# Rounding the second MLP's weights during attention, by way of DRAM, in an attention-and-two-MLPs kernel

## The chip, the cores and the metric

One core of one Trainium2 chip runs the whole kernel. The metric is device time in microseconds (us), the median of the runs shown. TensorE is called PE, VectorE DVE, ScalarE ACT, GpSimd POOL; SP is the queue of SyncE, which issues every DMA of this kernel.

## The reference

```python
# q, k, v: (4, 8, 768, 64) float32; chunks of 32 queries, 16 keys left, 8 keys right, 8 memory keys
scores = scale * np.matmul(q_c, k_full.transpose(0, 1, 3, 2))
a = softmax(scores)
out[:, :, c_start:c_end] = np.matmul(a, v_full)
x = out.transpose(0, 2, 1, 3).reshape(3072, 512)
h = np.maximum(np.maximum(x @ w1, x @ w2), x @ w3)     # d_ff 768
x = h @ w_out
h = x @ w_in                                           # d_ff 2048
g = np.where(h >= 1, h, np.where(h <= -1, 0, (h + 1) ** 2 / 4))
out = g @ w_out2
```

All six weight matrices are float64.

## The kernel before

**Work.** The 3072 tokens form 24 units of 128 for attention and 6 blocks of 512 (`TB`) for the products. Every product is made of float32r parts, hi and lo, as three matmuls (`mm3`, L467). One *slot* (l1, l2, l3 or l4) is 12 matmuls of 512 columns. The first MLP takes 24 slots a block: for each of six f, l1 with m = 0, l1 with m = 1, l2 of the f before, l1 with m = 2. An l1 result in one of two PSUM buffers is read by ACT for m = 0 (L492) and by DVE for m = 1, 2 (L494, `l1_max`); after m = 2, ACT makes hi (L477) and POOL lo (L478). The second MLP follows for all six blocks: 96 slots l3 (`slot_l3`) and 96 slots l4.

**Weights.** A float64 weight tile of 512 KB is fetched into one of three `st` buffers (`fetch_w`, L106) and converted: `convert_w` (L120) makes a float32 bit pattern from the upper word on DVE (L129 absolute value, L130 clamp, L131 shift and mask, L133 sign), `hi_w` rounds it to float32r on ACT (L140), `rest_w` (L143) takes the lower word's share on DVE (L146, L152), `lo_w` subtracts and adds on POOL (L159, L160). The 24 tiles of the first MLP ("a", "b") are converted in block 0, the 32 of the second ("c", "d") from the start of the last block on: `w_step` (L584) does one whole tile, in the loop over the last block's slots (L692) and before l3 slots (L706 to L710). The 48 weight buffers hold 24 tiles in hi and lo; 16 more are made where attention's buffers lay, once attention is done (L685).

**Order.** Units 0 to 7 and block 0 follow a list written out by hand. After that every engine's queue holds the program's order: for each slot of blocks 1 to 4 (96 slots) the slot itself, then one step of attention (`att_step`, L461). `steps` (L432 on) gives each unit u six steps: 0 scores and softmax start, 1 and 2 normalising and preparing keys and queries of later units, 3 transposing probabilities, 4 their product with v (`st_o`), 5 transposing the result into `xh`, `xl` (L410, L414). From unit 12 on keys and queries are transposed by DVE (`flip_k` L296, `flip_q` L302) from buffers that `load_ks` (L271) and `load_qs` (L286) fill three units at a time, with 20 and 16 DMAs; `load_v` fills the one buffer `vw` with 8 DMAs, in step 4. In units 12 and later a unit's step 2 is: `flip_k` of the next unit, `flip_q` of the one after that, then the loads.

```python
if last_block:
    t = s - last_block
    if t % 3 != 2 and converted[0] - 32 < t:
        w_step()
...
else:
    att_step()
```

Of the kernel before, what the change touches and what calls it, by code (L numbers as in the profile page):

```python
# [1 line left out]

# [16 lines left out]
P = 128  # L19
CH = 32          # queries per chunk  # L20
LEFT = 16        # context keys left of a chunk
RIGHT = 8        # context keys right of a chunk
NM = 8           # memory keys
WIN = LEFT + CH + RIGHT
NK = NM + WIN    # keys a chunk attends to
NC = P // CH     # chunks per unit of 128 tokens
TB = 512         # tokens per block
UB = TB // P     # units per block
FLOOR = -3.0e38
TRIO0 = 12       # first unit whose queries and keys the vector engine transposes  # L30
# float32 patterns of a float64's upper word at float32's smallest and largest exponents
LEAST, MOST = 2.0 ** -15, float.fromhex("0x1.dffffep+16")

# Order of the parts of units 0 to 7 and of block 0's products, by name and number: loads (lk lq lv
# lm lmem, f: weights), units (tk ck ek kw tq c0q c1q mem mv s mx ex n a ca o co x cx dx), weights (wa
# wh wg wp), products (l lt lh m), d: matrix products that only keep the tensor engine's clock up.
# The tensor engine follows it as it stands; it sets the priorities on the other engines.
# [18 lines left out]
# what the vector engine copies instead of ScalarE, and which steps go from it to another engine  # L56
# [11 lines left out]
def attention_then_two_mlps(ctx, tc, q, k, v, mem_k, mem_v, w1, w2, w3, w_mid, w_in, w_out, out):  # L68
# [4 lines left out]
    KD = DM // P          # 4  # L73
    K1 = F1 // P          # 6
    K2 = F2 // P          # 16
    HP = H // 2           # head pairs
    UPB = S // P          # units per batch
# [17 lines left out]
    yd = dram.tile([DM, NT], F32, name="yd")  # L95

    # ---------------------------------------------------------------- weights
    # A float64 weight comes as two 32-bit words.  It is kept as two float32r parts: `hi`
    # rounds the float32 that the upper word gives, `lo` holds the rest, the lower word's
    # share included.  # L100
# [19 lines left out]
    def convert_w(kind, j):  # L120
        st = staged.pop((kind, j))
        low, up = st[:, :, 0], st[:, :, 1]
        c = stage.tile([P, TB], U32, tag="c", name=f"c_{kind}_{j}")
        cf = c.bitcast(F32)
        V = nc.vector
        if f"{kind}.{j}" in ABS_ON_ACT:
            nc.scalar.activation(out=cf, in_=up.bitcast(F32), func=AF.Abs)
        else:
            V.tensor_scalar(out=c, in0=up, scalar1=0x7FFFFFFF, scalar2=None, op0=ALU.bitwise_and)  # L129
        V.tensor_scalar(out=cf, in0=cf, scalar1=LEAST, scalar2=MOST, op0=ALU.max, op1=ALU.min)  # L130
        V.tensor_scalar(out=c, in0=c, scalar1=3, scalar2=0x3FFFFFFF,  # L131
                        op0=ALU.logical_shift_left, op1=ALU.bitwise_and)
        V.scalar_tensor_tensor(out=c, in0=up, scalar=0xC0000000, in1=c,  # L133
                               op0=ALU.bitwise_and, op1=ALU.bitwise_or)
        half[kind, j] = low, up, c
# [26 lines left out]
    # ---------------------------------------------------------------- attention  # L162
    kTb = [at.tile([P, HP, LEFT + P + RIGHT], F32, name=f"kTb{i}") for i in range(2)]
# [93 lines left out]

    # From unit TRIO0 on, three units at a time, the loads put a head's parity and half of its
    # dims in a partition's quadrant, so that transposes of 32 x 32 blocks are all that is left.
    # Blocks of keys start LEFT tokens before a chunk.  # L260
    NB3 = 3 * NC
    ks = kq[:, 0:HP * (NB3 + 1) * CH].rearrange("p (h c d) -> p h c d", h=HP, d=CH)
    qs = {}

# [6 lines left out]
    def load_ks(g):  # L271
        b, s0 = divmod(3 * g, UPB)
        t0 = s0 * P - LEFT
        c0 = 1 if t0 < 0 else 0
        for h in range(HP):
            for r, a in quadrants(k[b], h, t0 + c0 * CH, CH, NB3):
                nc.sync.dma_start(out=ks[r:r + CH, h, c0:c0 + NB3, :], in_=a)
        r0, c, t = (LEFT, 0, 0) if c0 else (0, NB3, S - LEFT)
        for e in range(2):
            for x in range(2):  # L280
                r = (2 * e + x) * 32 + r0
                nc.sync.dma_start(
                    out=ks[r:r + LEFT, :, c, :],
                    in_=k[b].rearrange("(h e) t d -> e t h d", e=2)[e, t:t + LEFT, :, 32 * x:32 * x + 32])

    def load_qs(g):  # L286
        b, s0 = divmod(3 * g, UPB)
        for i in range(2):
            t = stage.tile([P, TB, 2], U32, tag="st", name=f"qs{g}_{i}", bufs=3)
            qs[g, i] = t.rearrange("p f t -> p (f t)").bitcast(F32)[:, 0:2 * NB3 * CH].rearrange(  # L290
                "p (h c d) -> p h c d", h=2, d=CH)
            for h in range(2):
                for r, a in quadrants(q[b], 2 * i + h, s0 * P, CH, NB3):
                    nc.sync.dma_start(out=qs[g, i][r:r + CH, h], in_=a)

    def flip_k(u):  # L296
        c = u % 3 * NC
        fill_mk(u)
        nc.vector.transpose(out=kw[:, :, :, NM:NM + CH], in_=ks[:, :, c:c + NC, :])
        nc.vector.transpose(out=kw[:, :, :, NM + CH:], in_=ks[:, :, c + 1:c + 1 + NC, :])  # L300

    def flip_q(u):  # L302
        c = u % 3 * NC
        for i in range(2):
            for e in range(2):
                r = slice(e * 64, e * 64 + 64)
                nc.vector.transpose(
                    out=qTb[u % 2][r, 2 * i:2 * i + 2, :, e, :], in_=qs[u // 3, i][r, :, c:c + NC, :])

    # the two heads of a pair lie on the diagonal of a block of queries  # L310
# [6 lines left out]
    # rows of a score tile: (chunk parity, head parity, query); columns: (chunk pair, head pair, key),  # L317
    # with the head pairs in the order 0, 2, 1, 3
# [51 lines left out]
    # heads g and g + 4 share the partitions of a transposed tile, g = 2 * (pair % 2) + parity  # L370
# [54 lines left out]
    def steps(u):  # L425
# [13 lines left out]
        if u >= TRIO0 - 3 and u % 3 == 0:  # L439
            v += [("gq", u // 3 + 1)]  # L440
# [7 lines left out]
        yield v + [("lv", u + 1)]  # L448
        yield [("x", u), ("cx", u), ("dx", u)]

    def run(kind, i):
        if kind in ("gk", "gq"):
            if i < NU // 3:
                parts[kind](i)
        elif kind in ("lm", "f", "d", "wa", "wh", "wg", "wp") or i < NU:
            parts[kind](i)
# [4 lines left out]
    def att_step():  # L461
        if todo:
            for s in todo.pop():
                run(*s)

    # ---------------------------------------------------------------- products
# [38 lines left out]
    def slot_l2(j, f):  # L505
        hi, lo = hs.pop(("A", j, f))
        whi, wlo = weights["b", f]
        for d in range(KD):
            if f == 0:
                acc[d] = ps_acc.tile([P, TB], F32, tag=f"acc{d}", name=f"y{j}_{d}")  # L510
            c = slice(d * P, (d + 1) * P)
            mm3(acc[d], whi[:, c], wlo[:, c], hi, lo, f == 0, f == K1 - 1)
            if f == K1 - 1:
                pool, tag = (mx, "y") if d < 2 else (bp["p"], "y") if bp else (stage, "c")
                y = pool.tile([P, TB], F32, tag=tag, name=f"y_{j}_{d}", bufs=2)
                nc.scalar.copy(out=y, in_=acc[d])
                nc.sync.dma_start(out=yd[d * P:(d + 1) * P, j * TB:(j + 1) * TB], in_=y)
# [16 lines left out]
    def slot_l3(i, f):  # L534
# [5 lines left out]
        # with u = max(h/2 + 1/2, 0) the gate is max(min(u, 1) * u, h)  # L540
# [26 lines left out]
    # ---------------------------------------------------------------- schedule  # L567
# [11 lines left out]
    def w_fetch():  # L579
        while fetched[0] < min(converted[0] + 3, len(conv)):  # L580
            fetch_w(*conv[fetched[0]][0])
            fetched[0] += 1

    def w_step():  # L584
        if converted[0] == len(conv):
            return
        w_fetch()
        n, pool = conv[converted[0]]
        pool = pool or bp["w"]
        convert_w(*n)  # L590
        hi_w(*n, pool)
        rest_w(*n)
        lo_w(*n)
        converted[0] += 1
        w_fetch()

    later = ExitStack()
    with tc.manual_schedule(engines={ENG.PE}), later:
# [8 lines left out]
        # what no load or copy writes of the buffers that stay  # L607
# [5 lines left out]
        # until the first products two buffers of later blocks serve, too  # L613
# [23 lines left out]
        # keeps the tensor engine's clock up while it waits for the first units  # L637
# [41 lines left out]
        for s, (f, *a) in enumerate(order):  # L679
# [9 lines left out]
            if last_block:  # L689
                t = s - last_block  # L690
                # a slot of the last block frees its weights' tiles
                if t % 3 != 2 and converted[0] - 32 < t:  # L692
# [8 lines left out]
            else:  # L701
                att_step()
        for f, *a in orderB:
            if f is slot_l3:
# [3 lines left out]
                if i == 0:  # L708
                    for _ in range({0: 0, 1: 0, 5: 2, 7: 2}.get(ff, 1)):
                        w_step()  # L710
# [39 lines left out]
```

## Time and profile before

| what | value |
|---|---|
| median of 3 runs | 1139.43 us (1139.12 to 1139.65) |
| span of the profiled execution, first to last instruction | 1136.8 us |
| its own time | it is not listed apart from the three runs; the median is 2.6 us over the span |
| PE busy | 1051.1 us, 92% of the span |
| DVE / ACT / POOL busy | 599.0 / 326.2 / 392.3 us |
| mean granted TensorE clock | 0.973 |

A busy share is a mean over stages: attention's head and block 0 (to about 170 us), blocks 1 to 4 with the rest of attention (to 479 us), the last block with the weight conversion (to about 700 us), and the second MLP. Matmuls overlap in the records, so the time of one slot is read from their starts and not from the sum of their durations.

### The profile page before, as it was taken

What the parts mean: (1) busy time and instruction counts of PE and PEld (TensorE: products, weight loads), DVE (VectorE), ACT (ScalarE), POOL (GpSimd) and SP (SyncE); (2) the same over time, 40 slices, a digit from 0 to 9 for tenths busy, and PEclk for the clock granted to TensorE, in tenths of its full rate; (3) what the DMA queues carried; (4) which work ended last, traced back from release to release, by engine and by line L of the source; (5) the groups of instructions that cost most, each with busy time, mean ns of one, the idle gap of its engine ahead of it and who ended that gap; (6) DMA issues with size and microseconds to landing.
All of it is one profiled execution on the core that took longest, in us unless ns stands there. A gap on an engine that the chain in (4) does not pass through costs nothing.

```text
span 1136.8 us, 15111 instructions
## 1 busy us (share of the span) xinstructions
PE 1051.1 (92%) x5890; PEld 848.2 (75%) x5890; DVE 599.0 (53%) x875; ACT 326.2 (29%) x608; POOL 392.3 (35%) x297
## 2 busy tenths in 40 slices
PE   5887789999999999987888779999999999999998
PEld 4765577888878888866666567888888888888886
DVE  8899963444435343399989996222222222222222
ACT  5734342232222222222132223222222222222222
POOL 5465650001000001166666664332332232232221
PEclk8998999999999999998988899999999999999999
DMA  8655423224233320243233221001001000000101
GB/s 203 171 135 139 111 67 87 52 42 91 44 60 80 57 73 18 71 138 104 93 109 104 84 65 47 19 10 47 10 19 47 10 19 29 28 10 1 37 1 37
DMA packets 154774, 72.94 MB, mean 64 GB/s; under 512 B 125264, under 2 KB 142672, under 8 KB 154704
## 3 DMA queue, kind: packets, MB, share of 16 engines
q1 hardware_dynamic: 154704, 71.99, 23.9%
q8 instruction: 46, 0.75, 0.3%
q14 instruction: 24, 0.20, 0.1%
HBM read 59.38 MB, written 12.58 MB: 63 GB/s over the span
## 4 chain that ended last, share of the span: by engine, by line
PE 69%; DVE 25%; issue 3%; DMA 1%; ACT 1%; POOL 0%; SPq 0%; DVEq 0%; POOLq 0%; ACTq 0%
PE l L468 13%; PE l L469 13%; PE l L470 13%; PE o L557 7%; PE o L556 7%; PE o L555 6%; PE y L468 2%; DVE u L543 2%; PE y L469 2%; PE y L470 2%; DVE c_d L130 2%; PE s L326 2%; DVE c_c L130 2%; PE o L389 2%; DVE c_d L129 1%
## 5 line engine op out<-in xcount | busy, mean ns | idle before, releaser
L543 DVE SCALAR_TENSOR_TENSOR u<-u 128x512 f32<-128x512 f32 x96 | 82.5, 859 | 316.0 <-ACT u L542 316.0
L478 POOL TENSOR_TENSOR hl_b<-u,hh_b 128x512 fp32r<-128x512 f32 x96 | 124.1, 1293 | 317.7 <-ACT hh_b L477 183.9
L468 PE MATMUL l<-xh,hi_a 128*128 128x512 f32 x432 | 178.0, 412 | 20.7 <-DVE t L494 20.7
L468 PE MATMUL l<-yh,hi_c 128*128 128x512 f32 x384 | 155.2, 404 | 26.3 <-DVE u L544 21.3
L470 PE MATMUL l<-xh,lo_a 128*128 128x512 f32 x432 | 171.3, 397 | 0.3 <-POOL lo_a L160 0.3
L469 PE MATMUL l<-xl,hi_a 128*128 128x512 f32 x432 | 171.0, 396 | 0.0
L469 PE MATMUL l<-yl,hi_c 128*128 128x512 f32 x384 | 153.8, 400 | 0.0
L470 PE MATMUL l<-yh,lo_c 128*128 128x512 f32 x384 | 153.7, 400 | 0.0
L555 PE MATMUL o<-hi_d,hh_b 128*128 128x512 f32 x384 | 150.0, 391 | 0.0
L557 PE MATMUL o<-hi_d,hl_b 128*128 128x512 f32 x384 | 150.0, 391 | 0.0
L556 PE MATMUL o<-lo_d,hh_b 128*128 128x512 f32 x384 | 149.9, 390 | 0.0
L478 POOL TENSOR_TENSOR hl_a<-t,hh_a 128x512 fp32r<-128x512 f32 x36 | 48.6, 1351 | 286.2 <-ACT hh_a L477 286.2
L542 ACT ACTIVATE u<-l 128x512 f32<-128x512 f32 x96 | 57.3, 596 | 204.3 <-PE l L470 168.8
L468 PEld LDWEIGHTS l<-xh,hi_a 128*128 128x128 f32 x432 | 83.1, 192 | 41.1 <-DVE t L494 24.5
L468 PEld LDWEIGHTS l<-yh,hi_c 128*128 128x128 f32 x384 | 73.9, 192 | 46.7 <-DVE u L544 25.4
L477 ACT CAST hh_b<-u 128x512 fp32r<-128x512 f32 x96 | 59.6, 621 | 158.5 <-DVE u L544 158.5
L494 DVE TENSOR_TENSOR t<-l,t 128x512 f32<-128x512 f32 x72 | 49.6, 689 | 104.1 <-PE l L470 99.8
L470 PEld LDWEIGHTS l<-xh,lo_a 128*128 128x128 f32 x432 | 82.6, 191 | 18.9 <-POOL lo_a L160 0.7
L469 PEld LDWEIGHTS l<-xl,hi_a 128*128 128x128 f32 x432 | 83.2, 193 | 15.7
L470 PEld LDWEIGHTS l<-yh,lo_c 128*128 128x128 f32 x384 | 74.3, 193 | 16.8
L469 PEld LDWEIGHTS l<-yl,hi_c 128*128 128x128 f32 x384 | 74.1, 193 | 16.0
L555 PEld LDWEIGHTS o<-hi_d,hh_b 128*128 128x128 f32 x384 | 72.5, 189 | 15.9
(136 smaller groups left out, 1538.4 us busy)
## 6 DMA issues: line engine op xcount, KB each, us to landing
st_a<-in_moe_w_dram SPq DMA_DIRECT2D x18, 512.0 KB
vw<-in_v_dram SPq DMA_DIRECT2D x160, 56.0 KB
st_c<-in_moe_w_in_dram SPq DMA_DIRECT2D x16, 512.0 KB
st_d<-in_moe_w_out_dram SPq DMA_DIRECT2D x16, 512.0 KB
yd<-y SPq DMA_DIRECT2D x24, 256.0 KB
yr<-yd SPq DMA_DIRECT2D x24, 256.0 KB
out_dram<-ob SPq DMA_DIRECT2D x24, 256.0 KB
kq<-in_q_dram SPq DMA_DIRECT2D x12, 256.0 KB
```

What stands on the lines that cost most here:

```text
L130: V.tensor_scalar(out=cf, in0=cf, scalar1=LEAST, scalar2=MOST, op0=ALU.max, op1=ALU.min)
L468: nc.tensor.matmul(ps, whi, xhi, start=first, stop=False)
L469: nc.tensor.matmul(ps, whi, xlo, start=False, stop=False)
L470: nc.tensor.matmul(ps, wlo, xhi, start=False, stop=last)
L477: nc.scalar.copy(out=hi, in_=h)
L478: nc.gpsimd.tensor_tensor(out=lo, in0=h, in1=hi.bitcast(F32), op=ALU.subtract)
L494: nc.vector.tensor_tensor(out=cur["t"], in0=ps, in1=cur["t"], op=ALU.max)
L542: nc.scalar.activation(out=a, in_=ps, func=AF.Relu, bias=0.5, scale=0.5)
L543: nc.vector.scalar_tensor_tensor(out=a, in0=a, scalar=1.0, in1=a, op0=ALU.min, op1=ALU.mult)
L555: nc.tensor.matmul(acc[t], hi[:, c], whi, start=first, stop=False)
L556: nc.tensor.matmul(acc[t], hi[:, c], wlo, start=False, stop=False)
L557: nc.tensor.matmul(acc[t], lo[:, c], whi, start=False, stop=last)
```

## The change

During blocks 1 to 4 each slot also runs `round_step`: a "c" or "d" tile is fetched at steps 0 and 2, `convert_w` runs at steps 3 and 5, and `round_w`, in the next step that allows it (4 and 0), adds the lower word's share, which gives a float32 weight. At steps 0 and 2 it is written to the DRAM tensor `wd` (256 KB a tile). In the last block and the first l3 slots `w_step` reads a tile back and splits it: hi on ACT, lo on DVE. The absolute value of "c" and "d" tiles moves from DVE to ACT. `hi_w`, `rest_w` and `lo_w` remain for block 0 alone. To share SP and the buffers, `load_ks` and `load_qs` now put their DMAs into a list, `queue`; `round_step` issues up to four DMAs a step from it (fewer where it writes and fetches, none at step 5), and a flip first issues all that is left. `load_qs` takes two units at a time (16 DMAs), from the second group on into the memory of the old `kTb` buffers instead of the `st` buffers. `load_v` moves to step 5. Two of the four copies `y` use the `hh` and `hl` buffers.

```diff
+    wd = dram.tile([2 * K2, P, TB], F32, name="wd")
...
-        if f"{kind}.{j}" in ABS_ON_ACT:
+        if kind in "cd" or f"{kind}.{j}" in ABS_ON_ACT:
             nc.scalar.activation(out=cf, in_=up.bitcast(F32), func=AF.Abs)
...
+    def round_w(kind, j):
+        low, up, c = half.pop((kind, j))
+        cf, upf = c.bitcast(F32), up.bitcast(F32)
+        V = nc.vector
+        V.tensor_scalar(out=up, in0=c, scalar1=0xFF800000, scalar2=None, op0=ALU.bitwise_and)
+        V.scalar_tensor_tensor(out=upf, in0=low, scalar=2.0 ** -52, in1=upf, op0=ALU.mult, op1=ALU.mult)
+        V.tensor_tensor(out=cf, in0=cf, in1=upf, op=ALU.add)
+        return cf
+
+    def load_w(n):
+        kind, j = conv[n][0]
+        staged[kind, j] = t = stage.tile([P, TB], F32, tag="st", name=f"w_{kind}_{j}", bufs=3)
+        nc.sync.dma_start(out=t, in_=wd[n - len(round1)])
+
+    def split_w(n, pool):
+        kind, j = conv[n][0]
+        t = staged.pop((kind, j))
+        hi = pool.tile([P, TB], F32R, tag="w", name=f"hi_{kind}_{j}")
+        lo = pool.tile([P, TB], F32R, tag="w", name=f"lo_{kind}_{j}")
+        nc.scalar.copy(out=hi, in_=t)
+        nc.vector.tensor_tensor(out=lo, in0=t, in1=hi.bitcast(F32), op=ALU.subtract)
+        weights[kind, j] = hi, lo
...
     def load_qs(g):
-        b, s0 = divmod(3 * g, UPB)
...
+        b, s0 = divmod(2 * g, UPB)
+        if 2 * g == TRIO0:
+            t = stage.tile([P, TB, 2], U32, tag="st", name=f"qs{g}", bufs=3)
+            t = t.rearrange("p f t -> p (f t)").bitcast(F32)
+        else:
+            t = kT2.rearrange("p i h t -> p (i h t)")[:, 0:2 * TB]
+        qs[g] = t.rearrange("p (h c d) -> p h c d", h=HP, d=CH)
+        for h in range(HP):
+            for r, a in quadrants(q[b], h, s0 * P, CH, 2 * NC):
+                queue.append(partial(nc.sync.dma_start, out=qs[g][r:r + CH, h], in_=a))
 
     def flip_k(u):
+        while queue:
+            queue.pop(0)()
...
     def flip_q(u):
...
+        while queue:
+            queue.pop(0)()
+        c = u % 2 * NC
+        for e in range(2):
+            r = slice(e * 64, e * 64 + 64)
+            nc.vector.transpose(out=qTb[u % 2][r, :, :, e, :], in_=qs[u // 2][r, :, c:c + NC, :])
...
-        if u >= TRIO0 - 3 and u % 3 == 0:
-            v += [("gq", u // 3 + 1)]
+        if u == TRIO0 - 3 or u >= TRIO0 - 1 and u % 2:
+            v += [("gq", (u + 3) // 2)]
...
-        yield v + [("lv", u + 1)]
-        yield [("x", u), ("cx", u), ("dx", u)]
+        yield v
+        yield [("x", u), ("cx", u), ("dx", u), ("lv", u + 1)]
...
+    stash, slot = [], [1]
+
+    def round_step():
+        at_step = slot[0] % 6
+        slot[0] += 1
+        room = 4
+        if at_step in (0, 2) and stash:
+            n, t = stash.pop(0)
+            nc.sync.dma_start(out=wd[n - len(round1)], in_=t)
+            room -= 1
+        if at_step in (0, 2) and fetched[0] < len(conv):
+            fetch_w(*conv[fetched[0]][0])
+            fetched[0] += 1
+            room -= 1
+        while queue and room > 0 and at_step != 5:
+            queue.pop(0)()
+            room -= 1
+        if at_step != 1 and at_step != 2 and converted[0] < fetched[0]:
+            n = converted[0]
+            name = conv[n][0]
+            if name in half:
+                stash.append((n, round_w(*name)))
+                converted[0] += 1
+            elif at_step in (3, 5):
+                convert_w(*name)
+
+    ready, asked = [len(round1)], [len(round1)]
+
     def w_step():
...
+        while asked[0] < min(ready[0] + 3, converted[0] - len(stash)):
+            load_w(asked[0])
+            asked[0] += 1
+        if ready[0] < asked[0]:
+            split_w(ready[0], conv[ready[0]][1] or bp["w"])
+            ready[0] += 1
...
-                if t % 3 != 2 and converted[0] - 32 < t:
+
+                if converted[0] < len(conv) or stash:
+                    round_step()
+                if ready[0] - 32 < t:
                     w_step()
...
             else:
                 att_step()
+                round_step()
...
                 if i == 0:
-                    for _ in range({0: 0, 1: 0, 5: 2, 7: 2}.get(ff, 1)):
-                        w_step()
+                    w_step()
```

## Rows read from the trace of the kernel before

**Rows 1.** The page's part 2: busy tenths in 40 slices of the span.

```profile
PE   5887789999999999987888779999999999999998
DVE  8899963444435343399989996222222222222222
PEclk8998999999999999998988899999999999999999
```

**Rows 2.** Busy time by stage: PE, PEld, DVE, ACT, POOL, granted clock, DMA share, GB/s.

```profile
170.00:479.00 309.00, 308.74 (x2248) 248.58 (x2247) 126.62 (x231) 78.79 (x136) 29.68 (x23) 1.00 0.28 63
479.00:720.00 241.00, 200.76 (x801) 157.77 (x800) 212.51 (x250) 60.63 (x106) 147.42 (x100) 0.93 0.28 88
720.00:1132.70 412.70, 412.67 (x1808) 339.01 (x1806) 109.30 (x159) 104.14 (x175) 116.60 (x91) 1.00 0.06 20
```

**Rows 3.** Waits of PE from 479 to 720 us: total, times, longest.

```profile
PE l L468 <- DVE u L544: 21.3, 8, 6.5
PE l L468 <- DVE t L494: 17.8, 6, 6.0
```

**Rows 4.** DVE's instructions by line from 490 to 700 us: busy us, mean ns.

```profile
L543 DVE SCALAR_TENSOR_TENSOR u<-u 128x512 f32<-128x512 f32 x18 | 28.5, 1583 | 6.5 <-ACT u L542 6.5
...
L130 DVE TENSOR_SCALAR c_d<-c_d 128x512 f32<-128x512 f32 x16 | 22.5, 1406 | 0.6
```

**Rows 5.** Timeline: the first converted tile of the second MLP, and POOL beside it.

```profile
480.62 0.43 DVE L130 TENSOR_SCALAR c_c<-c_c 128x512 f32<-128x512 f32 x1
...
481.05 1.28 POOL L478 TENSOR_TENSOR hl_a<-t,hh_a 128x512 fp32r<-128x512 f32 x1 [11.77 <-ACT hh_a L477]
481.08 1.53 DVE L131 TENSOR_SCALAR c_c<-c_c 128x512 uint32<-128x512 uint32 x1
...
482.65 0.69 DVE L133 SCALAR_TENSOR_TENSOR c_c<-st_c,c_c 128x512 uint32<-128x512 uint32 x1
...
483.38 0.43 DVE L146 TENSOR_SCALAR st_c<-c_c 128x512 uint32<-128x512 uint32 x1
...
483.84 0.69 DVE L152 SCALAR_TENSOR_TENSOR st_c<-st_c 128x512 f32<-128x512 uint32 x1
...
487.58 0.43 DVE L131 TENSOR_SCALAR c_c<-c_c 128x512 uint32<-128x512 uint32 x1
```

**Rows 6.** The tile c_a: ACT's absolute value, duration min/median/max in ns.

```profile
L127 ACT ACTIVATE c_a<-st_a x8: 662/676/702, 41.6 to 145.4; 128x512 f32<-128x512 f32 x8
```

**Rows 7.** The chain from 170 to 490 us: scores of units three apart.

```profile
400.27 1.08 PE s L326 x32
459.71 1.08 PE s L326 x32
```

**Rows 8.** Timeline of SP: start, us spent issuing, DMAs.

```profile
179.09 8.12 SPq L294 DMA_DIRECT2D qs<-in_q_dram  x16
195.54 3.55 SPq L217 DMA_DIRECT2D vw<-in_v_dram  x8
...
457.20 1.53 SPq L112 DMA_DIRECT2D st_c<-in_moe_w_in_dram  x3
```

**Rows 9.** Busy time by stretch (columns as in Rows 2), behind those three fetches.

```profile
459.00:461.00 2.00, 2.00 (x37) 1.54 (x36) 0.78 (x2) 0.00 (x0) 0.00 (x0) 1.00 1.00 328
461.00:463.00 2.00, 2.00 (x10) 1.61 (x10) 1.38 (x2) 0.55 (x1) 0.00 (x0) 1.00 1.07 363
463.00:465.00 2.00, 2.00 (x11) 1.65 (x10) 1.75 (x4) 0.09 (x1) 0.00 (x0) 1.00 0.15 48
```

**Rows 10.** Timeline of DVE: the flips of one unit's step 2.

```profile
308.61 0.70 DVE L299 STREAM_TRANSPOSE kw<-kq 128x512 f32<-128x512 f32 x1
309.23 0.67 DVE L300 STREAM_TRANSPOSE kw<-kq 128x512 f32<-128x512 f32 x1
309.83 1.77 DVE L307 STREAM_TRANSPOSE qTb<-qs 64x256 f32<-64x256 f32 x4
```

**Rows 11.** DMA issues of the key loads, ns min/median/max.

```profile
L277 SPq DMA_DIRECT2D kq<-in_k_dram x64: 311/467/612, 199.1 to 396.7; - x64
```

More of the change, by code (lines that the diff above doesn't have):

```diff
@@ L1 @@
 from contextlib import ExitStack
+from functools import partial
 import concourse.bass as bass
@@ L160, in lo_w @@
         nc.gpsimd.tensor_tensor(out=lo, in0=cf, in1=upf, op=ALU.add)
-    kTb = [at.tile([P, HP, LEFT + P + RIGHT], F32, name=f"kTb{i}") for i in range(2)]
+    def round_w(kind, j):
[18 more added lines that the diff above has]
+        weights[kind, j] = hi, lo
+    kT2 = at.tile([P, 2, HP, LEFT + P + RIGHT], F32, name="kT2")
+    kTb = [kT2[:, i] for i in range(2)]
     kw = at.tile([P, HP, NC, NK + RIGHT], F32, name="kw")
@@ L263, in attention_then_two_mlps @@
     qs = {}
+    queue = []
     def quadrants(src, h, t0, rows, n):
@@ L276, in load_ks @@
             for r, a in quadrants(k[b], h, t0 + c0 * CH, CH, NB3):
-                nc.sync.dma_start(out=ks[r:r + CH, h, c0:c0 + NB3, :], in_=a)
+                queue.append(partial(nc.sync.dma_start, out=ks[r:r + CH, h, c0:c0 + NB3, :], in_=a))
         r0, c, t = (LEFT, 0, 0) if c0 else (0, NB3, S - LEFT)
@@ L281, in load_ks @@
                 r = (2 * e + x) * 32 + r0
-                nc.sync.dma_start(
-                    out=ks[r:r + LEFT, :, c, :],
-                    in_=k[b].rearrange("(h e) t d -> e t h d", e=2)[e, t:t + LEFT, :, 32 * x:32 * x + 32])
+                queue.append(partial(
+                    nc.sync.dma_start, out=ks[r:r + LEFT, :, c, :],
+                    in_=k[b].rearrange("(h e) t d -> e t h d", e=2)[e, t:t + LEFT, :, 32 * x:32 * x + 32]))
     def load_qs(g):
-        b, s0 = divmod(3 * g, UPB)
[L288 to L294, printed above, removed]
+        b, s0 = divmod(2 * g, UPB)
[8 more added lines that the diff above has]
+                queue.append(partial(nc.sync.dma_start, out=qs[g][r:r + CH, h], in_=a))
     def flip_k(u):
+        while queue:
+            queue.pop(0)()
         c = u % 3 * NC
@@ L302, in flip_q @@
     def flip_q(u):
[L303 to L308, printed above, removed]
+        while queue:
[4 more added lines that the diff above has]
+            nc.vector.transpose(out=qTb[u % 2][r, :, :, e, :], in_=qs[u // 2][r, :, c:c + NC, :])
     def cp_q(u, e):
@@ L447, in steps @@
             v += [("mv", u + 1), ("lm", (u + 1) // UPB + 1)]
-        yield v + [("lv", u + 1)]
-        yield [("x", u), ("cx", u), ("dx", u)]
+        yield v
+        yield [("x", u), ("cx", u), ("dx", u), ("lv", u + 1)]
     def run(kind, i):
         if kind in ("gk", "gq"):
-            if i < NU // 3:
+            if i < NU // (3 if kind == "gk" else 2):
                 parts[kind](i)
@@ L461, in att_step @@
     def att_step():
-        if todo:
-            for s in todo.pop():
-                run(*s)
+        for s in todo.pop() if todo else ():
+            run(*s)
     def mm3(ps, whi, wlo, xhi, xlo, first, last):
@@ L513, in slot_l2 @@
             if f == K1 - 1:
-                pool, tag = (mx, "y") if d < 2 else (bp["p"], "y") if bp else (stage, "c")
-                y = pool.tile([P, TB], F32, tag=tag, name=f"y_{j}_{d}", bufs=2)
+                if d < 2 or bp:
+                    y = (mx if d < 2 else bp["p"]).tile([P, TB], F32, tag="y", name=f"y_{j}_{d}", bufs=2)
+                else:
+                    y = mx.tile([P, TB], F32, tag=("hh", "hl")[d % 2], name=f"y_{j}_{d}", bufs=3)
                 nc.scalar.copy(out=y, in_=acc[d])
@@ L577, in attention_then_two_mlps @@
     bp = {}
-    def w_fetch():
-        while fetched[0] < min(converted[0] + 3, len(conv)):
+    stash, slot = [], [1]
[8 more added lines that the diff above has]
+        if at_step in (0, 2) and fetched[0] < len(conv):
             fetch_w(*conv[fetched[0]][0])
             fetched[0] += 1
-    def w_step():
[L585 to L595, printed above, removed]
+            room -= 1
[11 more added lines that the diff above has]
+    ready, asked = [len(round1)], [len(round1)]
+    def w_step():
+        while asked[0] < min(ready[0] + 3, converted[0] - len(stash)):
[4 more added lines that the diff above has]
+            ready[0] += 1
     later = ExitStack()
```

## The prediction

> **What bounds the kernel now.** I read the slices of the span first: PE is at 9 except at the head and in slices 17 to 23, and there DVE is at 9 and the granted clock at 8 or 9 [rows 1]. Then busy time by stage. From 170 to 479 us (blocks 1 to 4 with the rest of attention) PE is busy 308.7 of 309 us, DVE only 126.6. From 479 to 720 us, where the second MLP's weights are converted, DVE is busy 212.5 of 241 us, POOL 147.4 and PE 200.8, at a clock of 0.93 [rows 2]. Third, PE's waits in that stage: 39.1 us, all for DVE, half for the gate of l3 and half for `l1_max` [rows 3]. The conversion stands in DVE's queue ahead of them: the clamp alone took 1406 ns, the gate's first step 1583 [rows 4].
>
> What that stage loses: behind it PE runs 1808 matmuls in 412.7 us, 0.2283 us each; the 801 of the stage would take 182.9 us at this pitch and took 241.0 [rows 2]. So **58 us** are to be had. The 39 us of waits are most of it; matmuls at the lower clock, 7% of 241 us or 17, are nearly all the rest. In the stages before and behind, where PE hardly stops, the clock stood at 1.00 [rows 2], so I count its share as won when the waits go.
>
> **The change part by part.**
>
> *Taken from the last block:* six DVE steps and two POOL steps a tile. In their place a tile costs a 256 KB read, an ACT copy and one DVE subtraction of 128x512 float32, about 0.69 us by L133 and L152, which have two SBUF operands, too [rows 5]. A slot is 12 x 0.2283 = 2.74 us of PE, and `w_step` splits at most one tile a slot: DVE has two such passes in it, 1.4 us. PE is the bound again, and the 58 us come back. The first splits wait for reads that SP issues only as `st` buffers come free; I take 1 us for this change of stage (bounds 0 and one slot, 3).
>
> *Added to blocks 1 to 4, DVE.* A tile is rounded by L130 0.43, L131 0.43, L133 0.69, the mask 0.43 (L146), L152 0.69 [rows 5] and the new addition, 0.69 by the same two rows: 3.36 us. Fetches at two of six steps in 96 slots are 32 tiles, of which the order rounds 31 before the last block: 104 us. The dear price stands there, too: an L131 that met a POOL subtraction took 1.53 us, the next one 0.43 [rows 5]. POOL runs 23 operations in this stage, 29.7 us [rows 2]; if each held up a DVE step for its whole length, that adds 30 us. DVE: 126.6 + 104 + at most 30 = 261 of 309 us, 84%. The 182 us that DVE idles now are the cover. Without it, as in the last block, PE would stop. Should the work bunch, the two PSUM buffers let an `l1_max` be a slot late; the heaviest step (0) adds 1.8 us of `round_w` to two passes over the scores, and the next rounding comes only at step 3. I take 2 us over the 96 slots; bounds nothing and, if each of 31 tiles cost PE a quarter of a slot, 21 us.
>
> The Trainium skill (SBUF — State Buffer, section "SBUF: two separate sides") calls the port pair that VectorE and GpSimd share an exclusive lock for a whole instruction, which blocks two-port steps and those with two SBUF inputs. That agrees with the 1.53 against 0.43 us. By that rule the new addition and the last block's subtraction can be blocked like the L131; its bearing is a rival below.
>
> *ACT.* The absolute value moves to it: 0.68 us [rows 6] x 32 = 22 us, on 78.8 busy of 309 [rows 2]. Hidden. DVE's clamp now waits for ACT behind that step's copy; this lies in the 2 us.
>
> *DMA data.* A unit of attention takes 59.44 / 3 = 19.8 us [rows 7]. In it come two more fetches (1 MB) and two writes (0.5 MB). Three fetches issued in 1.53 us [rows 8] filled the engines for about 4 us at 328 to 363 GB/s [rows 9], so 1.5 MB takes 4 to 5 us of a unit in which the engines are at 0.28 [rows 2]. Hidden: a tile is converted three steps after its fetch. A rounded tile leaves its buffer two or three steps before that is needed again.
>
> *SP's queue.* A small DMA costs SP 8.12 / 16 = 0.51 us, a `vw` load 0.44, a fetch 0.51 [rows 8]. Two units need 16 `vw` loads (7 us), 16 query loads and some 13 key loads (15 us), 4 fetches, 4 writes and about 3 `yd` writes (5 us): 27 of 39.6 us. It fits. Moving `load_v` to step 5 leaves it five steps until `st_o`, some 16 us, against 3.6 us of issue and a landing. The query loads for 2 units instead of 3 are in this sum.
>
> *The list of loads.* Between a unit's step 2 and the next unit's step 2, `round_step` issues 2 + 4 + 4 + 0 + 2 + 4 = 16 DMAs. Queries alone are 16: none is left. At u = 13 and u = 19 queries and keys come together, 36: twenty key loads are left for the moment before `flip_k` of units 15 and 21. SP can't do them earlier, because `load_v` stands in its queue and waits for `st_o` in step 4. From there SP needs 3.6 us for `vw`, 1.0 for a write and a fetch, 0.51 x (2 + 4 + 16) = 11.2 for the rest, about 2 for the landing (my estimate: [rows 9] show data still moving 4 us behind three issues of ten times the size): 17.8 us, and up to 2.5 more where SP comes late from step 4. DVE reaches the flip four steps behind `st_o`, 4/6 x 19.8 = 13.2 us. So DVE stands 4.6 to 7.1 us. Behind it are queued the two flips, 3.1 us [rows 10], a conversion's 1.55 and the next `l1_max`, 0.69. The slots there are l2, m = 2 and m = 0, which run 8.9 us without DVE; DVE needs 5.3 of them for its own queue, so 3.6 us are covered and PE loses 1.0 to 3.5 us. I take 2 us, twice: 4 us (bounds 0, and 14 with no cover).
>
> **Sum**, against the profiled execution: 1136.8 - 58 + 1 + 2 + 4 = 1085.8 us of span. The median stands 2.6 us above that span: **1088 us**.
>
> **The rivals.**
>
> *A clean win.* SP runs ahead, no flip waits, bunching costs nothing: 1136.8 - 58 + 2.6 = 1081 us. For it: PE's 308.7 of 309 us show no sensitivity to DVE's bursts now. Against: the count of twenty loads.
>
> *DVE bunches.* The rounding falls on POOL's splits, and its delay reaches `l1_max` and the split that l2 needs. By the lock of the Trainium skill's page this would be the rule rather than the exception. With 21 us instead of 2 and 10 instead of 4: 1113 us; half of that, 1100. For it: 1.41 us for the mean clamp of the last block [rows 4]. Against: POOL is busy 61% of that stage and 10% of this one [rows 2].
>
> *SP becomes the bound, and the kernel slower.* If the new traffic makes an issue dearer, each pair of units lasts as long as SP. The twelve units from 12 on are six pairs; to eat 51 us and 2.3 more (0.2% of the time, about what a measurement of this kernel tells from no change), a pair must last 39.6 + 8.9 = 48.5 us. With 5 us of large DMAs and 45 small ones that is 0.97 us an issue. The rows have 0.47 in the median and 0.61 at most [rows 11]. At 1.1 us it would be 54.5 us a pair, 36 more than at the break-even: about 1178 us.
>
> *The rounding doesn't get ahead.* It can't: the order of the queues is fixed by loops, and only one tile is left for the last block.
>
> **How the numbers follow.** The forecast (1083 to 1096) 0.6, the clean win 0.17, bunching 0.16, SP 0.04, and 0.03 for costs that cancel the gain. Up to 1104 the range takes in most of bunching; below, a pitch a little better than 0.2283 gives 1079. Left out are SP, the cancelling and the worst of bunching, about 0.13. Faster by over 0.2%: 0.93; within it 0.02; slower 0.05.
>
> **What would show it.** Right: from 170 us to the end PE at 9 in all slices, clock 1.00; DVE at 8 in blocks 1 to 4 and about 5 in the last block; the stage of the 801 matmuls at about 184 us; POOL without L159 and L160 there; a DVE wait for a key DMA before `flip_k` at units 15 and 21 alone. Wrong: PE waiting for `l1_max` in many slots of blocks 1 to 4, clamps at 1.4 us there, issues near 1 us, or DVE waiting for ACT's hi copy or a read of `wd` in the last block.

## The result and the profile after

The changed kernel takes 1091.56 us, the median of 4 runs from 1086.95 to 1094.32; the kernel before takes 1139.28 beside it. The ratio is 0.958, with a 95% interval from 0.9556 to 0.9604. The profiled execution took 1090.18 us, its span is 1088.1 us: 2.3 us over the 1085.8 of the sum. The median lies 3.2 us over the forecast before rounding (1085.8 + 2.6 = 1088.4): it stands 3.5 us above that span, not 2.6.

The slices of the span of the kernel after, to hold against [rows 1]:

```profile
PE   4887889999999999999999999999999999999998
DVE  8899984678578777666454232223223223223222
PEclk8998999999999999999999999999999999999999
```

Counted from 0, PE is at 9 from slice 6 to the last but one. DVE's load has moved ahead: in slices 7 to 16 it stands at 5 to 8, where it was 3 to 5, and in slices 17 to 23 at 2 to 6, where it was 8 or 9.

By stage (columns as in rows 2), blocks 1 to 4, then from the last block on:

```profile
170.00:479.00 309.00, 302.52 (x2178) 243.28 (x2177) 220.49 (x379) 93.62 (x162) 30.60 (x23) 0.99 0.52 135
479.00:720.00 241.00, 241.00 (x1087) 198.18 (x1086) 93.82 (x128) 76.97 (x135) 63.96 (x49) 1.00 0.22 68
```

Where PE was busy 200.8 of 241 us at a clock of 0.93 [rows 2], it is now busy all the time at 1.00, and POOL, which no longer splits weights there, is busy 64.0 us where it was 147.4. What PE lost before, it loses no more; instead it stops for 6 us in blocks 1 to 4, where it hardly did. Its waits from 170 to 1000 us, but for one of 0.3 us (total, times, longest):

```profile
PE tx L434 <- ACT xs L428: 6.2, 2, 3.6
```

The two stops lie from 290 to 320 us and from 410 to 440; the granted clock is 0.94 in both windows.

The products of a block end with the last matmul into `y`, so its start is a milestone of both kernels. Picked from PE's timeline of the kernel before, blocks 0 to 5 and then the last matmul of all:

```profile
169.74 0.39 PE L470 MATMUL y<-hh_a,lo_b 128*128 128x512 f32 x1
250.85 0.39 PE L470 MATMUL y<-hh_a,lo_b 128*128 128x512 f32 x1
330.11 0.39 PE L470 MATMUL y<-hh_a,lo_b 128*128 128x512 f32 x1
409.36 0.39 PE L470 MATMUL y<-hh_a,lo_b 128*128 128x512 f32 x1
487.30 0.39 PE L470 MATMUL y<-hh_a,lo_b 128*128 128x512 f32 x1
580.61 0.39 PE L470 MATMUL y<-hh_a,lo_b 128*128 128x512 f32 x1
1132.28 0.39 PE L557 MATMUL o<-hi_d,hl_b 128*128 128x512 f32 x1
```

The same rows of the kernel after:

```profile
169.75 0.39 PE L501 MATMUL y<-hh_a,lo_b 128*128 128x512 f32 x1
250.95 0.39 PE L501 MATMUL y<-hh_a,lo_b 128*128 128x512 f32 x1
335.35 0.39 PE L501 MATMUL y<-hh_a,lo_b 128*128 128x512 f32 x1
414.60 0.39 PE L501 MATMUL y<-hh_a,lo_b 128*128 128x512 f32 x1
496.67 0.39 PE L501 MATMUL y<-hh_a,lo_b 128*128 128x512 f32 x1
562.15 0.39 PE L501 MATMUL y<-hh_a,lo_b 128*128 128x512 f32 x1
1083.23 0.39 PE L590 MATMUL o<-hi_d,hl_b 128*128 128x512 f32 x1
```

The last block shrank from 93.3 to 65.5 us, 27.8 less. What follows it, to the last matmul, shrank from 551.7 to 521.1, 30.6 less. Blocks 1 and 3 are unchanged to 0.1 us (81.1 and 81.2; 79.2 and 79.2). Block 2 grew from 79.3 to 84.4, block 4 from 77.9 to 82.1. So 58.4 us were won, 9.3 given back.

The place where they are given back, in the kernel after: SP's issues ahead of unit 15's key flip,

```profile
275.86 4.45 SPq L244 DMA_DIRECT2D vw<-in_v_dram  x8
...
281.27 3.19 SPq L628 DMA_DIRECT2D kT<-in_q_dram  x6
284.50 12.04 SPq L328 DMA_DIRECT2D kq<-in_k_dram  x20
```

and DVE's timeline over the same time:

```profile
288.35 0.69 DVE L525 TENSOR_TENSOR t<-l,t 128x512 f32<-128x512 f32 x1 [0.61 <-PE l L501]
295.63 0.71 DVE L331 STREAM_TRANSPOSE kw<-kq 128x512 f32<-128x512 f32 x1 [6.58 <-DMA kq<-in_k_dram]
...
299.80 0.68 DVE L525 TENSOR_TENSOR t<-l,t 128x512 f32<-128x512 f32 x1
```

Twenty key loads come last, and the flip waits 6.58 us for them. The `l1_max` behind it ends at 300.5. ACT's timeline, and under it PE's:

```profile
300.52 0.62 ACT L508 CAST hh_a<-t 128x512 fp32r<-128x512 f32 x1 [7.87 <-DVE t L525]
301.04 0.58 ACT L428 COPY xs<-o 128x512 f32<-128x512 f32 x1
```

```profile
297.72 0.39 PE L501 MATMUL l<-xh,lo_a 128*128 128x512 f32 x1
301.67 1.12 PE L434 MATMUL tx<-ident,xs 128*128 128x128 f32 x4 [3.56 <-ACT xs L428]
```

ACT stands 7.87 us at the hi part of that `l1_max`; queued behind it is the copy of the attention output, `xs`, whose product ended at 295.2. PE stops 3.56 us for this copy. And the granted clock is low when it starts again (busy times in stretches of 4 us; the clock is the third number from the end, where 1.00 is the upper of its two levels, 2.4 GHz, and a number below it a mean over the stretch):

```profile
296.00:300.00 4.00, 2.11 (x10) 1.41 (x8) 3.88 (x8) 0.00 (x0) 0.00 (x0) 1.00 0.60 172
300.00:304.00 4.00, 2.33 (x8) 2.04 (x9) 3.71 (x5) 2.76 (x5) 1.40 (x1) 0.65 0.62 142
304.00:308.00 4.00, 4.00 (x44) 3.16 (x43) 2.69 (x6) 0.00 (x0) 0.00 (x0) 0.92 0.59 197
```

Block 2 is 5.1 us longer than before: 3.6 of it is the stop. The other 1.6 I put down to the clock, which from the last two rows comes to about (0.35 + 0.08) x 4 = 1.7 us. At unit 21 the same chain stops PE for 2.6 us after a key wait of 5.6, and block 4 is 4.1 us longer.

### The profile page after: what moved, and what is told of

The parts are those of the page before. It is cut to its first block, busy times and chain, and to the rows that moved or that the text cites. A ratio compares the mean times of both kernels' runs of the same rounds, so it can differ in the third digit from the quotient of the medians.

```text
span 1088.1 us, 15214 instructions
## 1 busy us (share of the span) xinstructions
PE 1034.8 (95%) x5890; PEld 841.9 (77%) x5890; DVE 561.9 (52%) x883; ACT 344.3 (32%) x640; POOL 292.9 (27%) x233
## 4 chain that ended last, share of the span: by engine, by line
PE 82%; DVE 11%; issue 2%; DMA 2%; SPq 2%; ACT 1%; POOL 0%; DVEq 0%; ACTq 0%; POOLq 0%
PE l L499 15%; PE l L500 15%; PE l L501 15%; PE o L590 8%; PE o L589 8%; PE o L588 8%; PE y L499 3%; PE y L500 2%; PE y L501 2%; PE s L358 2%; PE o L421 1%; DVE c_a L132 1%; DVE c_a L135 1%; SPq L328 1%; DMA st_d<-in_moe_w_out_dram 1%
## 5 line engine op out<-in xcount | busy, mean ns | idle before, releaser
L576 DVE SCALAR_TENSOR_TENSOR u<-u 128x512 f32<-128x512 f32 x96 | 66.5, 692 | 357.4 <-ACT u L575 357.4
L499 PE MATMUL l<-yh,hi_c 128*128 128x512 f32 x384 | 150.5, 392 | 0.0
L500 PE MATMUL l<-yl,hi_c 128*128 128x512 f32 x384 | 150.4, 392 | 0.0
L501 PE MATMUL l<-yh,lo_c 128*128 128x512 f32 x384 | 150.3, 391 | 0.0
L590 PEld LDWEIGHTS o<-hi_d,hl_b 128*128 128x128 f32 x384 | 72.1, 188 | 15.5
```

The costliest lines, as they stand in the source:

```text
L499: nc.tensor.matmul(ps, whi, xhi, start=first, stop=False)
L500: nc.tensor.matmul(ps, whi, xlo, start=False, stop=False)
L501: nc.tensor.matmul(ps, wlo, xhi, start=False, stop=last)
L576: nc.vector.scalar_tensor_tensor(out=a, in0=a, scalar=1.0, in1=a, op0=ALU.min, op1=ALU.mult)
L590: nc.tensor.matmul(acc[t], lo[:, c], whi, start=False, stop=last)
```

## The experiments

Each is a change to the kernel after, but for e7. The kernel before, beside them, took 1139.06 to 1140.34 us in the median of each batch.

**e1: the loads in time.** Both units of a pair of query loads are flipped in the odd unit's step 2, keys go on the list first, and a key flip issues only what the keys still need.

```diff
-        if u + 2 >= TRIO0:
-            v += [("fq", u + 2)]
+        if u + 2 >= TRIO0 and u % 2:
+            v += [("fq", u + 1), ("fq", u + 2)]
...
     def flip_k(u):
-        while queue:
+        while any(p.keywords["out"].tensor is ks.tensor for p in queue):
             queue.pop(0)()
```

> Both units of a query pair are flipped together in the odd unit's step 2, so queries have two units of time to arrive; keys are put on the list ahead of queries, and a key flip issues only what is left of the keys. Theory (two key flips wait for loads that SP issues last, and nothing else is lost in blocks 1 to 4): DVE's 14.6 us of waits for key DMAs fall below 2 us, PE is busy 30.0 of 30 us in every window from 200 us on, clock 1.00 there, and about 9 us go (6.2 us of PE stops, 2 to 3 us of matmuls at the lower clock behind them): 1081 to 1084 us. Rival (SP or the DMA engines are overloaded in general, the two flips are only where it shows): the waits turn up at other places and the time stays within 3 us of 1091.6.

Measured: 1082.06 us (1080.53 to 1083.21), ratio 0.949 [0.9471, 0.9508]. Its busy time from 200 to 600 us, and DVE's one wait for keys:

```profile
200.00:600.00 400.00, 400.00 (x2559) 324.49 (x2558) 269.18 (x439) 132.00 (x230) 57.52 (x43) 1.00 0.49 130
```

```profile
DVE kw L331 <- DMA kq<-in_k_dram: 2.7, 1, 2.7
```

PE is busy 400.00 of 400 us at clock 1.00, though one wait of 2.7 us is left where I had said below 2 in all. The two waits cost 9.5 us together by the medians and 9.3 by the milestones: by these, blocks 2 and 4 take 79.3 and 77.9 us here, as in the kernel before. SP and the DMA engines carry the same traffic as before this edit (136 and 135 GB/s from 170 to 479 us), so a general overload is out.

The executions spread over 2.7 us, and a difference of that size lies in block 0, which no edit here touches: its milestone stands at 172.41 us in e1's trace, at 169.75 in that of the kernel after, and between 169.7 and 172.6 in all traces. Why block 0 varies was not looked at. From that milestone to the last matmul e1, e6, e8 and e9 take 904.2 us each, the kernel after 913.5. So where medians differ by no more than 3 us, this stretch of the traces is given as well.

**e2: who hands the wait on.** Where l1 with m = 2 meets step 4, ACT copies `xs` first and makes hi of the slot behind it.

```diff
+            late = f is slot_l1 and a[2] == 2 and not last_block and slot[0] % 6 == 4
+            if late:
+                l1_pe(*a)
+                l1_max(*a)
+            else:
+                f(*a)
...
                 att_step()
+                if late:
+                    l1_split(*a)
                 round_step()
```

> Where an l1 slot with m = 2 meets a unit's step 4, ACT makes hi of the slot only behind the copy of the attention output; the loads stay as they are. DVE's waits for key DMAs stay at 6.6 and 5.6 us. Theory (both ACT's queue and the second PSUM buffer hand the wait on; the buffer's bound lies about 1.5 us below ACT's): the transposes no longer wait for the attention copy, PE waits for l1_max instead, 2.0 and 1.2 us, and the time falls by 3 to 4 us to about 1088. Rival (only ACT's queue hands it on, PSUM covers the rest): PE does not stop, about 1082 us. Rival (ACT's place is irrelevant): unchanged, 1091.

Measured: 1086.71 us (1085.21 to 1088.39), ratio 0.9527 [0.9508, 0.9546]. PE's waits from 170 to 600 us, but for the same one of 0.3 us, and DVE's for keys:

```profile
PE l L499 <- DVE t L525: 2.8, 2, 2.7
```

```profile
DVE kw L331 <- DMA kq<-in_k_dram: 14.2, 3, 7.2
```

DVE waits for keys as long as before, but PE stops for 2.8 us in place of 6.2, and now for `l1_max`; the time fell by 4.9 us (4.5 behind block 0), a little more than the 3 to 4 expected. So two lines lead from the flip to PE: ACT's queue, and behind it the PSUM buffers. The prediction priced the second alone.

**e3: no spreading.** The limit of four DMAs a step becomes 40, so the list goes out in the step that fills it.

```diff
-        room = 4
+        room = 40
```

> The list of loads is emptied in the step that fills it, without the limit of four DMAs a step. Theory (SP's capacity between two flips is short at units 13 and 19, whatever the order): SP issues 36 loads before that unit's v loads, which come 10 us later; DVE still waits 3 to 8 us for keys at two flips and PE may also wait for v: 1088 to 1098 us. Rival (spreading the loads makes the wait): no DVE wait for keys over 1 us, 1081 to 1084 us.

Measured: 1097.21 us (1096.17 to 1098.8), ratio 0.9624 [0.9608, 0.9641]: the time that the theory gave, in the main by another wait than the one for keys that it named; PE's waits for v, which it thought possible, come to 1.6 us from 170 us on. SP's issues, then what DVE and ACT waited for from 280 to 330 us:

```profile
271.49 7.74 SPq L628 DMA_DIRECT2D kT<-in_q_dram  x16
279.28 11.77 SPq L628 DMA_DIRECT2D kq<-in_k_dram  x20
291.14 3.58 SPq L244 DMA_DIRECT2D vw<-in_v_dram  x8
294.82 0.35 SPq L621 DMA_DIRECT2D wd<-c_d  x1
295.22 0.43 SPq L112 DMA_DIRECT2D st_d<-in_moe_w_out_dram  x1
```

```profile
DVE c_d L132 <- ACT c_d L129: 9.7, 2, 8.5
...
DVE kw L331 <- DMA kq<-in_k_dram: 1.2, 1, 1.2
```

```profile
ACT c_d L129 <- DMA st_d<-in_moe_w_out_dram: 8.6, 1, 8.6
```

The keys are nearly in time (1.2 us). But the fetch of the next weight tile is issued only at 295.2, behind 36 loads and `vw`, so ACT's absolute value waits for its data, DVE's clamp for ACT, and everything queued behind both. From 271.5 to 295.7 SP needs 24.2 us for what stands there, and a unit has 19.8: it can't issue all of it between two flips of such a unit, and spreading only chooses what is late.

**e4: does DVE have the cover?** Two more steps a tile that change nothing.

```diff
+        for _ in range(2):
+            V.tensor_tensor(out=upf, in0=upf, in1=upf, op=ALU.max)
         V.tensor_tensor(out=cf, in0=cf, in1=upf, op=ALU.add)
```

> Each rounding does two more DVE steps of 128x512 float32 with two SBUF operands that change nothing (a maximum of a tile with itself): 2 x 0.69 x 31 = 43 us more DVE work in blocks 1 to 4, from 72% to about 86% busy there. Theory (DVE's idle time covers the rounding): PE still busy in all windows but the two with the key waits, where the longer queue behind the flip adds up to 1.4 us each: 1091 to 1096 us. Rival (rounding steps bunch ahead of l1_max): PE loses at least a third of what is added, 1105 us or more.

Measured: 1097.01 us (1096.22 to 1098.2), ratio 0.9622 [0.9607, 0.9638], 1 us over what the theory gave and far from the rival's 1105. PE's waits from 170 to 600 us, but for the same one of 0.3 us:

```profile
PE tx L436 <- ACT xs L430: 9.6, 2, 5.7
```

They lie at the same two flips, where DVE waits 8.0 and 6.0 us for keys: PE stops 9.6 us there in place of 6.2, and the clock in the two windows of 30 us is 0.89 in place of 0.94.

**e5: the same without the two waits** (e4's edit on e1).

> The two DVE steps of e4_two_more on top of e1_flip_later. Theory (the 5.5 us that e4 cost all came from the two key waits, the rest of blocks 1 to 4 has the cover): PE busy 30.0 of 30 us in every window from 200 us on although DVE is busy about 26 of 30, and the time stays within 1.5 us of e1: 1081 to 1083.5. Rival (DVE at 86% already delays l1_max elsewhere, e1's margin hid it): 1085 us or more.

Measured: 1084.76 us (1083.24 to 1086.51), ratio 0.9513 [0.9496, 0.953], 2.7 us over e1 (3.4 behind block 0), between the two expectations. DVE is busy 262.8 of 309 us from 170 to 479 (85%), and 2.4 us go in one window:

```profile
350.00:380.00 30.00, 27.64 (x207) 21.65 (x205) 24.72 (x45) 9.28 (x16) 2.58 (x2) 1.00 0.48 118
```

```profile
DVE kw L333 <- DMA kq<-in_k_dram: 4.1, 1, 4.1
```

It begins with the third key wait, 4.1 us ahead of unit 18's flip, which the four last key loads of that group cause; with DVE this full the delay reaches PE 12 and 20 us later, as stops of 0.95 and 1.41 us.

**e6: the absolute value back on DVE** (on e1).

```diff
-        if kind in "cd" or f"{kind}.{j}" in ABS_ON_ACT:
+        if f"{kind}.{j}" in ABS_ON_ACT:
```

> e1_flip_later with the absolute value of the second MLP's tiles back on DVE: DVE gets 13 us (32 x 0.42), ACT loses 22, and DVE's waits of some 20 us for ACT's absolute value go. Theory (either engine has the cover): within 1.5 us of e1, 1081 to 1083.5. Rival (moving it to ACT was needed): DVE delays l1_max, 1085 us or more.

Measured: 1080.48 us (1080.13 to 1080.81), ratio 0.948 [0.9466, 0.9494]. DVE is busy 241.1 of 309 us and PE 400.00 of 400 from 200 us on. Behind block 0 it takes as long as e1. The move to ACT was not needed.

**e7: how much of the 58 us is DVE's alone.** On the kernel *before*, three DVE steps are left out for the second MLP's tiles.

```diff
+        if kind not in "cd":
             V.tensor_scalar(out=cf, in0=cf, scalar1=LEAST, scalar2=MOST, op0=ALU.max, op1=ALU.min)
...
```

> The kernel before, with the clamp, the shift and the sign step left out for the second MLP's tiles (their numbers are other ones); nothing is moved to blocks 1 to 4. DVE's 212.5 us from 479 to 720 us lose 30 x (1.40 + 0.85 + 0.76) = 90 us and POOL keeps its work. Theory (that stage lost 58 us to DVE alone, clock included): PE is busy there all the time at clock 1.00 and the time is 1139.4 - 58 = 1081 to 1085 us. Rival (POOL at 147 of 241 us or the fetches bind next): PE still waits, 1095 us or more.

Measured: 1089.91 us (1089.13 to 1092.74), ratio 0.9567 [0.9548, 0.9586], between the two expectations. The stage of the conversion, and DVE's two steps that are left over from 480 to 700 us:

```profile
479.00:720.00 241.00, 235.11 (x1018) 189.87 (x1017) 172.47 (x172) 72.99 (x128) 166.46 (x113) 1.00 0.29 91
```

```profile
L147 DVE TENSOR_SCALAR st_d<-c_d 128x512 uint32<-128x512 uint32 x16 | 23.8, 1489 | 0.6
L153 DVE SCALAR_TENSOR_TENSOR st_c<-st_c 128x512 f32<-128x512 uint32 x16 | 20.1, 1258 | 0.5
```

About half of the 90 us comes back, because the steps that stay now meet POOL: for the 32 tiles the mask takes 23.8 + 19.4 = 43.2 us, where it took 6.9 + 6.9 = 13.8 from 480 to 700 us (0.43 us each, as in [rows 5]), and L153 20.1 + 16.0 = 36.1 us where L152 took 22.2. POOL is busy 166 us of the stage. PE's idle time shrinks from 40 us to 6, and the clock is 1.00. So leaving out three DVE steps wins back 49 of the 58 us. The other 9 stand beside what is left of PE's waits, 4.7 us of them for the gate of l3 on DVE. The change takes POOL's subtractions out as well, by splitting on ACT and DVE; that they are what the 9 us hang on is argued and not shown, as no run takes them out alone.

**e8: e1 and e2 together.**

> e1_flip_later and e2_act_order together. Theory (ACT's order mattered only as it handed on the waits of the two flips, which e1 has taken away): within 1.5 us of e1, 1081 to 1083.5. Rival (ACT's order gains by itself): e2's 5 us come on top, 1077 us.

Measured: 1080.94 us (1080.45 to 1082.8), ratio 0.9487 [0.9471, 0.9503]. ACT's order gains nothing once the waits have gone.

**e9 and e10: five DMAs a step,** on e1 and on e5, to take the third wait away.

```diff
-        room = 4
+        room = 5
```

> e1_flip_later with five DMAs a step from the list instead of four, so that the 20 key loads of a group fit between two flips (3 + 5 + 5 + 0 + 3 + 5 = 21) and no four of them are left for the flip. Theory: the last key wait (2.7 us in e1, ahead of unit 18's flip, covered there) falls below 0.5 us; PE already never stops in e1, so the time stays that of e1, 1080 to 1082.5. Rival (list DMAs bunched ahead of the v loads delay those): PE waits for v, 1084 us or more.

> The same with the two further DVE steps a tile of e4. Theory (in e5 the 2.7 us went behind the one key wait that was left, 4.1 us at unit 18, and not because DVE at 86% is late by itself): without that wait PE stops for less than 0.7 us in blocks 1 to 4 and the time is within 1 us of e9. Rival (DVE at 86% is late by itself): 2 us or more over e9.

Measured: 1081.48 us (1080.97 to 1083.78), ratio 0.9496 [0.9483, 0.9509], and 1082.72 us (1082.38 to 1083.46), ratio 0.9505 [0.9492, 0.9518]. DVE's key waits, e9's and under it e10's:

```profile
DVE kw L331 <- DMA kq<-in_k_dram: 1.6, 1, 1.6
```

```profile
DVE kw L333 <- DMA kq<-in_k_dram: 2.5, 1, 2.5
```

The third wait got shorter and did not go, so that expectation failed: the last key load leaves SP about 1 us earlier (351.0 in place of 352.0 us), and still not early enough. e10 is 1.2 us over e9 (1.7 behind block 0), between its two expectations, and PE's stops of 1.4 us (0.3 in e9) are over the 0.7 expected. The comparison serves all the same. With a key wait of 2.5 us in place of 4.1, the 43 us of further DVE work cost 1.2 us instead of 2.7, and in e4, with waits of 8.0 and 6.0, 5.5 (behind block 0: 1.7, 3.4 and 6.4). So the price of a fuller DVE grew with the late loads: at 85% it has less of the reserve with which the queues absorb one. That 85% costs nothing without any late load is not shown, as no run with the further work is free of key waits.

The best versions are e1, e6, e8 and e9, 1080.5 to 1082.1 us; these runs do not rank them, and behind block 0 their traces agree to 0.05 us.

## Why the prediction was nearly right

**The 58 us of the last stage** came back whole. The milestones have it, 27.8 in the last block and 30.6 behind it; e1 against the kernel before is 58.3 us (1140.34 to 1082.06). The clock's share came with the waits, as assumed. The step that named DVE as the bound was not complete: in e7 DVE's other steps got longer beside POOL, and 49 of the 58 us came back. The change takes POOL's subtractions out of that stage, too, which the prediction listed and did not count.

**DVE in blocks 1 to 4.** Predicted 3.36 us a tile and up to 30 us of collisions; the six groups of lines sum to 3.5 us for a "c" tile and 3.9 for a "d" tile. The difference is in the addition, which takes 0.69 us for "c" tiles and more for "d" tiles (DVE's lines from 170 to 479 us):

```profile
L171 DVE TENSOR_TENSOR c_d<-c_d,st_d 128x512 f32<-128x512 f32 x13 | 15.8, 1215 | 0.4
```

Of the 13 additions for "d" tiles seven took 1.65 to 1.67 us and six 0.69. Each of the seven starts about 0.3 us behind the start of a split on POOL, as here, and none of the six beside one:

```profile
301.28 1.40 POOL L509 TENSOR_TENSOR hl_a<-t,hh_a 128x512 fp32r<-128x512 f32 x1 [17.04 <-ACT hh_a L508]
```

```profile
301.58 1.65 DVE L171 TENSOR_TENSOR c_d<-c_d,st_d 128x512 f32<-128x512 f32 x1
```

The Trainium skill (SBUF — State Buffer, section "SBUF: two separate sides") says that a VectorE step with two SBUF inputs and a GpSimd step that reads SBUF can't hold the shared port pair at once: the one that starts first keeps it for its whole instruction. The trace agrees: 0.69 us where POOL is idle, 1.65 beside its split. Bunching, the 2 us I took and the 21 I allowed, cost nothing: in e1 PE doesn't stop from 200 us on.

**The change of stage**, 1 us, cost nothing either: PE has no wait from 479 to 720 us.

**The list of loads** is the step that failed in size. The wait of DVE was right in mechanism, place and length: twenty key loads ahead of units 15 and 21, DVE waits of 6.6 and 5.6 us against 4.6 to 7.1. How it reaches PE was not, and four things were missed:

- The price taken was 2 us each, near the middle of the range of 1.0 to 3.5, while PE stopped for 3.6 and 2.6. The loads took SP 0.60 and 0.56 us apiece instead of 0.51, and the first wait came to the upper end.
- PE was stopped by ACT's queue, which I had not followed. By that way 3.0 us of a wait are covered (6.58 - 3.56 and 5.61 - 2.59) and not 3.6; with ACT's order changed (e2) the stops are 2.7 and 0.1 us after waits of 7.2 and 4.8, and about 4.6 are covered.
- A stop costs more than itself, as the clock is lower behind it: some 1.6 us in block 2 and 1.5 in block 4. Together 9.3 us instead of 4.
- A third, small wait (2.4 us, unit 18) I had excluded, though my own count of 16 issues leaves four of the 20 key loads when they come without queries, too; it was covered.

So the sum, corrected: 1136.8 - 58.4 + 9.3 = 1087.7 us of span, against 1088.1; most of the 0.4 left lies behind the last matmul. The forecast took 5.3 us too little for the list and 3 too much for bunching and the change of stage. That these two errors went opposite ways was luck, and it made the sum look better than its terms; the 0.9 us by which the median stands farther above the profiled span makes up the rest of the miss.

**The rivals.** Bunching didn't come: POOL's splits met seven of the 29 additions from 170 to 479 us, and PE never stopped for it in e1. SP as the bound of all units didn't come: e1 has the same traffic at full PE speed. Still, SP was the scarce resource, in two units of twelve, and the point of break-even in dearer issues was the wrong way to ask for it; the count of issues between two gates was the right one. The clean win at 1081 is what e1 is.

## What to carry to other kernels

Here work moved into an engine's idle time almost for nothing as long as nothing else was late. What it uses up is the reserve that absorbs late loads, so a spread-out list of loads needs a check of what is left for the moment of use, counted in issues between the two events that gate the queue. A wait on one in-order engine is handed on by the next engine's queue, so price a stall along every queue that stands behind it, and look in the trace for what the clock loses after the stop. When one engine is the bound of a stage, look which other engine lengthens its steps before counting its whole busy time as the price.

## What the runs showed of the hardware that I had not expected

PE's stop of 3.56 us ends at 301.7 us. The granted clock was 1.00 from 296 to 300 us, 0.65 in the next 4 us and 0.92 in the 4 behind them. For the stop of 2.59 us, which ends at 424.7, it was 0.76 from 422 to 426 and 0.81 in the 4 us behind them. e5's two shorter stops of 0.95 and 1.41 us left it at 1.00 in every stretch of 4 us around them. And leaving out some of DVE's steps made others longer: with three of them gone in e7, the mean of the mask for "d" tiles went from 0.43 to 1.49 us beside POOL.
